# XCiT attention and RWKV channel mix on one core: crossbar transposes for v, q and k, norms as row sums, one buffer for x, a tanh gate

## Chip, cores, metric

The kernel runs on one core of a Trainium2 chip. The metric is the device time of one execution in microseconds; the time before is the median of three runs. A profile is one execution recorded by the hardware profiler. Engines are called PE (TensorE, matmuls; PEld its weight loads), DVE (VectorE), ACT (ScalarE), POOL (GpSimd) and SP (SyncE, which here only issues DMAs). The 16 DMA engines serve the queues of all of them.

## What is computed

Two stages. The first is a cross-covariance attention over channels: the norms and the product k^T q run over all 6208 tokens, and the softmax is only 256 by 256 per batch. Its output x = v a goes through a channel mix with a shift by one token.

```python
B, N, C = 4, 6208, 256                      # d_ff = 1024, tau = 1.0, float32 in and out
qn = q / (norm(q, axis=1) + 1e-6)           # a norm per channel, over all tokens
kn = k / (norm(k, axis=1) + 1e-6)
s  = kn.T @ qn / tau                        # per batch, 256 x 256
a  = softmax(s, -1)
x  = v @ a                                  # 6208 x 256

x_prev = x shifted down by one token (first row zero)
xk = mu_k * x + (1 - mu_k) * x_prev
xr = mu_r * x + (1 - mu_r) * x_prev
kk = relu(xk @ w_k) ** 2
out = sigmoid(xr @ w_r) * (kk @ w_v)
```

## The kernel before

**Tiling.** Tokens are cut into 12 blocks of 512 per batch (NB = 12, M = 512, S = 4 pieces of 128); 64 tokens per batch are left over (L = 64) and make one last block of 256 columns ("left"). There are 49 blocks in all. Matmuls take bf16 and accumulate in PSUM. Everything after the attention is held transposed, channels in partitions and tokens along the free dimension, so v must be transposed: x^T = a^T v^T.

**Norms and covariance.** For q and k a *group* g is 512 tokens of both, and a *unit* is 128 tokens of a group. `unit_matmul` (L115) adds a unit's k^T q into s_ps with two matmuls (L125). The squares of q and k are made on ACT (L113, or L108 for batch 0) and summed over tokens by matmuls with a matrix of ones, four at a time on strips of 32 columns (L131). `softmax_pieces` (L135) gathers the four strips with one more float32 matmul (L151), takes Sqrt on ACT (L152) and reciprocals on DVE (L156, L163), scales s, subtracts the row maximum, applies Exp with a sum as a second output (L177) and writes a_sb (L183). These eight pieces are put into the loop one per slot.

**Batch 0** is loaded in float32 on SP's queue (`group_load`, L86), q and k alternating, cast on DVE (L106) and squared on ACT (L108). Batches 1 to 3 are loaded by GpSimd's queue, which casts to bf16 (L100).

**The loop.** Blocks pass through a software pipeline. The loop over i from -2 to 48 has eight slots j; the order in which a slot issues its work is the order on each engine (the schedule is manual). In slot j of step i:

- `up(i + 1, j)`: two matmuls into kT_ps (L285) and a Relu to kr on ACT (L288); `square` (L294) makes kk on DVE one slot later.
- `down(i, j)`: for each 128 tokens the gate xr w_r (L309) and kk w_v (L313) into one vr_ps; `finish` applies Sigmoid on ACT (L321), multiplies on DVE (L322) and, after the fourth piece, SP stores 512 KB (L326).
- `x_half(i + 2, ...)` in slots 0 and 2: x^T (L230), copied to bf16 by ACT (L232). The tile xT has 513 columns; GpSimd copies the last column of the block before into the first (L225).
- `mix_delta`, `mix`: x - x_prev (L260), xk and xr (L270) on DVE.
- `v_load(i + 5)` on GpSimd's queue (L201); `v_transpose(i + 3)` in slot 6, eight PE transposes (L209); `v_evac` in slot 7, a DVE copy (L214).
- a `unit` of the next batch in slots 1, 3, 4, 5 and 7, until that batch's 49 units are done.

PSUM's eight banks: s_ps, ssq_ps, vT_ps, xT_ps, two kT_ps, two vr_ps.

Of the kernel before, what the change touches and what calls it, by code (L numbers as in the profile page):

```python
# [14 lines left out]
OP = mybir.AluOpType  # L15
# [3 lines left out]
def kernel(  # L19
# [23 lines left out]
    assert 0 < L < P  # L43
    G = NB * S
    inv_tau = 1.0 / float(tau)

# [3 lines left out]
    p2 = ctx.enter_context(tc.tile_pool(name="p2", bufs=3))  # L50
    ps = ctx.enter_context(tc.tile_pool(name="ps", bufs=1, space=bass.MemoryType.PSUM))
    ctx.enter_context(tc.manual_schedule())

# [4 lines left out]
    ones = const.tile([P, P], BF16, name="ones")  # L58
    nc.vector.memset(ones, 1.0)

    thirty2 = const.tile([P, P], F32, name="thirty2")
    nc.vector.memset(thirty2, 1.0 / 32)
# [6 lines left out]
    a_sb = const.tile([P, B, 2, C], BF16, name="a_sb")  # L69
    gate = const.tile([P, 1], BF16, name="gate")  # L70

    cov = {}
    groups = {}
# [4 lines left out]
    def qk_src(t, b, g):  # L81
        if g < NB:
            return t[b, :NB * M, :].rearrange("(p j) c -> p j c", p=P)[:, g * S:(g + 1) * S, :]
        return t[b, NB * M:, :].rearrange("(p j) c -> p j c", j=1)

    def group_load(b, g):  # L86
        rows, n = rows_of(g)
        qk = pq.tile([P, S, 2, C], BF16, name="qk", tag="qk", bufs=5)
        qk2 = pq.tile([P, S, 2, C], BF16, name="qk2", tag="qk2", bufs=3)
        groups[b, g] = (qk, qk2)  # L90
        if b == 0:
            t_f = []
            for i, t in enumerate((q, k)):
                f = pq.tile([P, S, C], F32, name=f"f{i}", tag=f"f{i}", bufs=6)
                nc.sync.dma_start(f[:rows, :n], qk_src(t, b, g))
                t_f.append(f)
            groups[b, g] += tuple(t_f)
        else:
            for i, t in enumerate((q, k)):
                nc.gpsimd.dma_start(qk[:rows, :n, i, :], qk_src(t, b, g))  # L100

    def group_cast(b, g):
        rows, n = rows_of(g)
        qk, qk2, *t_f = groups[b, g]
        for i in range(2):
            nc.vector.tensor_copy(qk[:rows, :n, i, :], t_f[i][:rows, :n])  # L106
        for i in range(2):
            nc.scalar.activation(qk2[:rows, :n, i, :], t_f[i][:rows, :n], AF.Square)  # L108

    def unit_square(b, g, s):  # L110
        rows, _ = rows_of(g)
        qk, qk2 = groups[b, g][:2]
        nc.scalar.activation(qk2[:rows, s], qk[:rows, s], AF.Square)  # L113

    def unit_matmul(b, g, s):  # L115
        rows, n = rows_of(g)
        t0 = g == 0 and s == 0
        te = g == NB
        if t0:
            cov[b] = (ps.tile([P, 2, C], F32, name="s_ps", tag="s_ps"),  # L120
                      ps.tile([P, 2 * C], F32, name="ssq_ps", tag="ssq_ps"))
        s_ps, ssq_ps = cov[b]
        qk, qk2 = groups[b, g][:2]
        for ih in range(2):
            nc.tensor.matmul(s_ps[:, ih, :], qk[:rows, s, 1, ih * P:(ih + 1) * P],  # L125
                             qk[:rows, s, 0, :], start=t0 and ih == 0, stop=te,
                             skip_group_check=True)

        if s == n - 1:
            for u in range(n):  # L130
                nc.tensor.matmul(ssq_ps[32 * u:32 * (u + 1)], ones[:rows, :32],  # L131
                                 qk2[:rows, u].rearrange("p i c -> p (i c)"),
                                 start=g == 0, stop=te if u == 0 else g == NB - 1, tile_position=(0, 32 * u))

    def softmax_pieces(b):  # L135

        s_ps, ssq_ps = cov.pop(b)
        nrm = pn.tile([P, 2 * C], F32, name="nrm")
        junk = pn.tile([P, P], F32, name="junk")
        rk = pn.tile([P, 2], F32, name="rk")  # L140
        rq = pn.tile([P, C], F32, name="rq")
        s_sb = pn.tile([P, 2, C], F32, name="s_sb")
        mx = pn.tile([P, 2], F32, name="mx")
        sm = pn.tile([P, 2], F32, name="sm")

        def a():
            nc.vector.tensor_copy(nrm, ssq_ps)

        def a2():
            all_ps = ps.tile([P, 2 * C], F32, name="all_ps", tag="ssq_ps")  # L150
            nc.tensor.matmul(all_ps, thirty2, nrm, start=True, stop=True)  # L151
            nc.scalar.activation(nrm, all_ps, AF.Sqrt)  # L152

        def b1():
            nc.vector.tensor_scalar_add(nrm[:, :C], nrm[:, :C], 1e-6)
            nc.vector.reciprocal(rq, nrm[:, :C])  # L156

        def b2():
            for ih in range(2):
                nc.vector.scalar_tensor_tensor(junk, nrm[:, C + ih * P:C + (ih + 1) * P], 1.0, ident_f,  # L160
                                               op0=OP.mult, op1=OP.mult, accum_out=rk[:, ih:ih + 1])
            nc.vector.tensor_scalar_add(rk, rk, 1e-6)
            nc.vector.reciprocal(rk, rk)  # L163
            if inv_tau != 1.0:
                nc.vector.tensor_scalar_mul(rk, rk, inv_tau)
# [310 lines left out]
```

## Time and profile before

| | |
|---|---|
| median of three runs | 581.26 us (578.61 to 582.14) |
| span of the profiled execution | 579.8 us |
| PE busy | 528.0 us (91%) |
| ACT busy | 451.7 us (78%) |
| DVE busy | 443.6 us (77%) |
| POOL busy | 126.9 us (22%) |
| DMA, queue q0 (GpSimd's, casting) | 32.98 MB, 46.3% of 16 engines' span |
| DMA, queue q1 (SP's) | 38.15 MB, 18.4% |
| mean granted PE clock | 0.975 |

The profiled execution's time is known by its span, from the first to the last instruction. Busy time is the time with at least one instruction of the engine under way; matmuls overlap, so a step in starts, not the length of one, tells what they cost. A view in order of time has start, length, engine, line, operation and tiles; in brackets stands idle time ahead of it and what ended that. Bytes of q0 are counted as written, in bf16; it reads twice as many.

### The profile page before, as it was taken

What the parts mean: (1) busy time and instruction counts of PE and PEld (TensorE: products, weight loads), DVE (VectorE), ACT (ScalarE), POOL (GpSimd) and SP (SyncE); (2) the same over time, 40 slices, a digit from 0 to 9 for tenths busy, and PEclk for the clock granted to TensorE, in tenths of its full rate; (3) what the DMA queues carried; (4) which work ended last, traced back from release to release, by engine and by line L of the source; (5) the groups of instructions that cost most, each with busy time, mean ns of one, the idle gap of its engine ahead of it and who ended that gap; (6) DMA issues with size and microseconds to landing.
All of it is one profiled execution on the core that took longest, in us unless ns stands there. A gap on an engine that the chain in (4) does not pass through costs nothing.

```text
span 579.8 us, 10793 instructions
## 1 busy us (share of the span) xinstructions
PE 528.0 (91%) x3920; PEld 350.9 (61%) x3920; DVE 443.6 (77%) x977; ACT 451.7 (78%) x895; POOL 126.9 (22%) x188
## 2 busy tenths in 40 slices
PE   4574999999889999999979999999979999999996
PEld 2331466666546666666646666666646666666765
DVE  4535788777798777777888777786789898888984
ACT  6845888888878888788887888887877777767774
POOL 0064233223121324313202323321101111110000
PEclk9955999999989999999999999999999999999999
DMA  8999979858538888957729687964222444522122
GB/s 329 415 267 196 135 111 143 151 84 124 102 54 151 129 145 130 133 110 109 111 55 183 93 130 127 148 103 100 57 54 58 108 73 94 105 60 73 37 74 90
DMA packets 95684, 71.80 MB, mean 124 GB/s; under 512 B 3980, under 2 KB 92304, under 8 KB 95632
## 3 DMA queue, kind: packets, MB, share of 16 engines
q0 software_dynamic: 65808, 32.98, 46.3%
q1 hardware_dynamic: 29824, 38.15, 18.4%
q8 instruction: 30, 0.49, 0.3%
q14 instruction: 22, 0.18, 0.1%
HBM read 78.65 MB, written 25.43 MB: 180 GB/s over the span
## 4 chain that ended last, share of the span: by engine, by line
PE 80%; DVE 9%; DMA 6%; ACT 3%; issue 1%; SPq 0%; ACTq 0%; DVEq 0%
PE kT_ps L285 27%; PE vr_ps L313 27%; PE xT_ps L230 7%; PE vr_ps L309 7%; PE s_ps L125 5%; PE vT_ps L209 4%; PE ssq_ps L131 2%; DMA f_185<-in_k_dram 2%; DMA f_273<-in_k_dram 2%; DVE kk L294 2%; DMA f_347<-in_k_dram 2%; DVE xk L270 1%; DVE rq L156 1%; DVE res L322 1%; ACT kr L288 1%
## 5 line engine op out<-in xcount | busy, mean ns | idle before, releaser
L288 ACT ACTIVATE kr<-kT_ps 128x512 bf16<-128x512 f32 (+1 forms) x392 | 232.8, 596 | 55.9 <-PE kT_ps L285 22.7
L313 PE MATMUL vr_ps<-w_v_sb,kk 128*128 128x256 bf16 x1552 | 233.8, 273 | 7.2 <-DVE kk L294 7.0
L285 PE MATMUL kT_ps<-xk,w_k_sb 128*128 128x512 bf16 (+1 forms) x784 | 232.9, 379 | 5.1 <-ACT kr L288 4.0
L313 PEld LDWEIGHTS <-kk 128*128 128x128 bf16 x1552 | 152.1, 98 | 66.6 <-DVE kk L294 8.3
L294 DVE TENSOR_TENSOR kk<-kr 128x512 bf16<-128x512 bf16 (+1 forms) x392 | 153.0, 417 | 1.9 <-ACT kr L288 1.4
L322 DVE TENSOR_TENSOR res<-res,vr_ps 128x256 f32<-128x256 f32 x194 | 81.6, 421 | 82.2 <-ACT res L321 81.8
L285 PEld LDWEIGHTS <-w_k_sb 128*128 128x128 bf16 x784 | 71.7, 98 | 44.1 <-issue 17.1
L125 PE MATMUL s_ps<-qk 128*128 128x256 bf16 x392 | 73.0, 287 | 18.3 <-DVE qk L106 18.3
L232 ACT CAST xT<-xT_ps 128x512 bf16<-128x512 f32 x96 | 56.5, 588 | 35.3 <-PE xT_ps L230 35.3
L321 ACT ACTIVATE res<-vr_ps 128x256 f32<-128x256 f32 x194 | 74.2, 382 | 7.6 <-PE vr_ps L313 7.1
L225 POOL COPY xT<-xT 128x2 bf16<-128x2 bf16 x44 | 28.0, 637 | 221.7 <-issue 174.0
L309 PE MATMUL vr_ps<-w_r_sb,xr 128*128 128x256 bf16 x388 | 74.2, 273 | 0.0
L270 DVE SCALAR_TENSOR_TENSOR xr<-delta,mu_r_t,xT 128x512 bf16<-128x512 bf16 x96 | 71.8, 748 | 0.0
L270 DVE SCALAR_TENSOR_TENSOR xk<-delta,mu_k_t,xT 128x512 bf16<-128x512 bf16 x96 | 71.6, 747 | 0.0
L230 PE MATMUL xT_ps<-vT,a_sb 128*128 128x512 bf16 x192 | 58.2, 385 | 11.2 <-DVE a_sb L183 7.8
L309 PEld LDWEIGHTS <-xr 128*128 128x128 bf16 x388 | 38.0, 98 | 44.9 <-issue 0.6
L201 POOL DMA_DIRECT2D v_bf<-in_v_dram x48 | 36.3, 757 | 113.8 <-DVE kk L294 92.1
L125 PEld LDWEIGHTS <-qk 128*128 128x128 bf16 x392 | 38.6, 102 | 31.4 <-DVE qk L106 22.1
L260 DVE TENSOR_TENSOR delta<-xT 128x1024 bf16<-128x1024 bf16 x48 | 33.3, 693 | 20.1 <-ACT xT L232 19.4
L100 POOL DMA_DIRECT2D qk<-in_q_dram x39 | 29.1, 747 | 52.9 <-PE s_ps L125 10.9
L214 DVE COPY vT<-vT_ps 128x1024 bf16<-128x1024 bf16 x48 | 32.9, 686 | 4.0 <-PE vT_ps L209 4.0
L209 PE MATMUL vT_ps<-ident,v_bf 128*128 128x128 bf16 x384 | 30.1, 223 | 0.8 <-DVE vT L214 0.8
(192 smaller groups left out, 313.7 us busy)
## 6 DMA issues: line engine op xcount, KB each, us to landing
out_dram<-res SPq DMA_DIRECT2D x48, 512.0 KB, 3.8
v_bf<-in_v_dram POOLq DMA_DIRECT2D x48, 256.0 KB, 4.4
qk<-in_q_dram POOLq DMA_DIRECT2D x36, 256.0 KB, 4.6
qk<-in_k_dram POOLq DMA_DIRECT2D x36, 256.0 KB, 6.4
f_93<-in_q_dram SPq DMA_DIRECT2D x1, 512.0 KB, 3.8
f_95<-in_k_dram SPq DMA_DIRECT2D x1, 512.0 KB, 4.8
f_117<-in_q_dram SPq DMA_DIRECT2D x1, 512.0 KB, 5.6
f_119<-in_k_dram SPq DMA_DIRECT2D x1, 512.0 KB, 6.7
```

What stands on the lines that cost most here:

```text
L125: nc.tensor.matmul(s_ps[:, ih, :], qk[:rows, s, 1, ih * P:(ih + 1) * P], qk[:rows, s, 0, :], start=t0 and ih == 0, stop=te, skip_group_che ...
L209: nc.tensor.transpose(vT_ps[:, ch, s * P:(s + 1) * P], v_bf[:, s, ch * P:(ch + 1) * P], ident)
L230: nc.tensor.matmul(xT_ps, a_sb[:, b, ih, dh * P:(dh + 1) * P], vT[:, ih, :], start=ih == 0, stop=ih == 1)
L232: nc.scalar.copy(xT[:, dh, 1:], xT_ps)
L270: nc.vector.scalar_tensor_tensor(o[:, dh], st[i, "d"][:, dh], mu[:, dh:dh + 1], st[i, "x"][:, dh, :M], op0=OP.mult, op1=OP.add)
L285: nc.tensor.matmul(kT_ps[:, :m], w_k_sb[:, dh, fh * P:(fh + 1) * P], xk[:, dh, :m], start=dh == 0, stop=dh == 1)
L288: nc.scalar.activation(kr[:, :m], kT_ps[:, :m], AF.Relu)
L294: nc.vector.tensor_tensor(st[i, "kk"][:, fh, :m], kr[:, :m], kr[:, :m], op=OP.mult)
L309: nc.tensor.matmul(vr_ps[:, D:], xr[:, dh, s * P:(s + 1) * P], w_r_sb[:, dh, :], start=dh == 0, stop=dh == 1)
L313: nc.tensor.matmul(vr_ps[:, :D], kk[:, fh, s * P:(s + 1) * P], w_v_sb[:, fh, :], start=fh == 0, stop=fh == 7)
L321: nc.scalar.activation(res[:, s], vr_ps[:, D:], AF.Sigmoid)
L322: nc.vector.tensor_tensor(res[:, s], res[:, s], vr_ps[:, :D], op=OP.mult)
```

## The change

The whole kernel body is rearranged around five edits; the arithmetic of the channel mix is the same.

1. **Transposes by DMA.** v blocks 2 to 47 are transposed from SBUF to SBUF with `dma_start_transpose` on SP's queue (`v_transpose_dma`, slot 1 of step i for block i + 4) and not on PE; `v_evac` is gone. Blocks 0 and 1 still use PE, with a DVE copy. q and k of batches 1 to 3 are transposed the same way, 128 x 2048 at a time (`group_transpose`), one group ahead of its first unit, and the left-over tokens of v too.
2. **Norms as row sums.** With channels in partitions, the sum over tokens of a unit is one ACT Square with `accum_out` over 128 x 512 elements. The matmuls with ones go for batches 1 to 3. The square root is a `pow` on GpSimd, the reciprocal is taken on 128 x 4 numbers, and q's factors come into the free dimension by a store to DRAM and a broadcast load. The row maximum is not subtracted (for |1/tau| up to 60); k's factor is the scale of Exp. s_ps is copied out by ACT when the batch's last unit is in.
3. **x of a batch in one buffer X**, 128 x 2 x 6145, so the column before a block is there already.
4. **Tanh gate.** sigmoid(z) = (1 + tanh(z/2))/2; the half is multiplied into w_v_sb once, on DVE. The gate has a PSUM bank of its own (g_ps), Tanh works on two pieces (128 x 512) at a time, and the finish is one scalar_tensor_tensor per two pieces.
5. **Batch 0's order.** q first, then q and k interleaved, k's last piece in parts of 2, 1 and 1; norms by matmuls with one column of ones; q's factor is ready before the last k pieces; v of block 0 comes in float32 on SP's queue.

The units are placed by a table `due`: the 49 units of batch 1 over 61 slots from step 0, those of batches 2 and 3 over 96 slots each. PSUM after: one bank for xT, g and s, two for v, three for kT. Output tiles share eight buffers (f4) with the float32 loads; v_bf, vT and batch 0's q share thirteen (b2).

The core of the diff:

```diff
+    X = const.tile([P, 2, 1 + NB * M], BF16, name="X")
+    nc.vector.memset(X[:, :, 0:1], 0.0)
...
+    def root(src, n):
+        a = pn.tile([P, 4], F32, name="nrm_a")
+        if len(src.shape) == 3:
+            nc.vector.tensor_reduce(a[:, :n], src, axis=AX, op=OP.add)
+        else:
+            nc.vector.tensor_copy(a[:, :n], src)
+        r = pn.tile([P, 4], F32, name="nrm_r")
+        nc.gpsimd.tensor_tensor(r[:, :n], a[:, :n], half[:, :n], op=OP.pow)
+        return r
...
+    def v_transpose_dma(i):
         v_bf = st.pop((i, "v"))
-        vT_ps = ps.tile([P, 2, M], BF16, name="vT_ps", tag="vT_ps")
-        for ch in range(2):
-            for s in range(S):
-                nc.tensor.transpose(vT_ps[:, ch, s * P:(s + 1) * P], v_bf[:, s, ch * P:(ch + 1) * P], ident)
-        st[i, "vTp"] = vT_ps
-
-    def v_evac(i):
-        vT = p2.tile([P, 2, M], BF16, name="vT", tag="vT", bufs=2)
-        nc.vector.tensor_copy(vT, st.pop((i, "vTp")))
-        st[i, "vT"] = vT
+        vT = new_vT(i)
+        nc.sync.dma_start_transpose(vT.rearrange("p s h t -> p (s h) t"), v_bf.rearrange("p s c -> p (s c)"))
...
-        nc.scalar.copy(xT[:, dh, 1:], xT_ps)
+        nc.scalar.copy(X[:, dh, 1 + t * M:1 + (t + 1) * M], xT_ps)
...
+    def gate_act(i, u):
+
+        if (i, "g", u) in st:
+            nc.scalar.activation(st[i, "res"][:, 2 * u:2 * u + 2], st.pop((i, "g", u)), AF.Tanh, scale=0.5)
...
-        nc.scalar.activation(res[:, s], vr_ps[:, D:], AF.Sigmoid)
-        nc.vector.tensor_tensor(res[:, s], res[:, s], vr_ps[:, :D], op=OP.mult)
...
+        nc.vector.scalar_tensor_tensor(r, r, 1.0, st.pop((i, "v", u)), op0=OP.add, op1=OP.mult)
...
+    def group_transpose(b, g):
+
+        rows, n = rows_of(g)
+        qk = groups[b, g]["qk"]
+        T = pq.tile([P, 2, S, 2, P], BF16, name="qkT", tag="qkT", bufs=3)
+        groups[b, g]["T"] = T
+        if n == S:
+            nc.sync.dma_start_transpose(T.rearrange("p i s h t -> p (i s h) t"), qk.rearrange("p i s c -> p (i s c)"))
...
+    def unit(b, g, s):
...
+        for ih in range(2):
+            nc.tensor.matmul(cov[b][:, ih, :], qk[:rows, 1, s, ih * P:(ih + 1) * P], qk[:rows, 0, s, :],
...
+        for u in ([s] if n == S else range(S)):
+            i, h = divmod(u, 2)
+            junk = pn.tile([P, S, P], BF16, name="junk")
+            nc.scalar.activation(junk[:, :n, :rows], G["T"][:, i, :n, h, :rows], AF.Square,
+                                 accum_out=ssq[b][:, u, g:g + 1])
...
+        def bcast_out():
+            d = pd.tile([2, P], F32, name="rq_d")
+            hold["d"] = d
+            with nc.allow_non_contiguous_dma(reason="256 words"):
+                nc.sync.dma_start(d.rearrange("h p -> p h"), hold["r"][:, 0:2])
+
+        def bcast_in():
+            rq_bc = pn.tile([P, C], F32, name="rq_bc", bufs=1)
+            hold["bc"] = rq_bc
+            nc.sync.dma_start(rq_bc, hold["d"].rearrange("h p -> (h p)").unsqueeze(0).to_broadcast([P, C]))
...
+        return [a, None, a2, bcast_out, bcast_in, None, None, None, None, c, e, None, f]
...
+    for ih in range(2):
+        soft_half(0, ih, t_sb, rk, e_sb, sm, mx)
+    v_load(1)
     nc.gpsimd.dma_start(w_r_sb, moe_w_r.rearrange("(ko ki) d -> ki ko d", ki=P))
     nc.gpsimd.dma_start(w_v_sb, moe_w_v.rearrange("(fo fi) d -> fi fo d", fi=P))
+    nc.vector.tensor_scalar_mul(w_v_sb, w_v_sb, 0.5)
     v_load(2)
...
+    for h in range(2):
+        v_transpose_pe(0, v0, 2 * h, 2 * h + 2, "v")
+    for ih in range(2):
+        soft_scale(0, ih, e_sb, sm)
...
+            if j == 1 and 2 <= i + 4 < LAST:
+                v_transpose_dma(i + 4)
+            if j == 2 and 3 <= i + 5 < LAST:
                 v_load(i + 5)
...
+            for u in due.get(T, []):
+                b, g, s = units[u]
+                at = (b - 1) * (NB + 1) + GORD.index(g)
+                while pos["load"] < min(len(loads), at + 4):
+                    group_load(*loads[pos["load"]])
+                    pos["load"] += 1
+                while pos["T"] < min(len(loads), at + 2):
+                    group_transpose(*loads[pos["T"]])
+                    pos["T"] += 1
+                unit(b, g, s)
```

## The prediction, on record before the change was run

> **What bounds the kernel now.** I read the page first, then the busy times by stage, then the up-projection's matmuls by stage, then single instructions in order of time, then the DMA queues. Lines of the page, with the profiled execution's span of 579.8 us in its head:
>
> ```profile
> PE 528.0 (91%) x3920; PEld 350.9 (61%) x3920; DVE 443.6 (77%) x977; ACT 451.7 (78%) x895; POOL 126.9 (22%) x188
> ...
> PE   4574999999889999999979999999979999999996
> ...
> ACT  6845888888878888788887888887877777767774
> ...
> PEclk9955999999989999999999999999999999999999
> ...
> PE 80%; DVE 9%; DMA 6%; ACT 3%; issue 1%; SPq 0%; ACTq 0%; DVEq 0%
> ```
>
> TensorE holds 80% of the chain of waits at the full granted clock, except in a head of some 66 us (clock 0.5 in slices 3 and 4) and in three dips. Busy time by stage (columns: us; busy us and instructions of PE, PEld, DVE, ACT, POOL; clock; DMA share; GB/s):
>
> ```profile
> 80.00:140.00 60.00, 58.90 (x456) 39.97 (x457) 44.86 (x98) 50.05 (x106) 18.51 (x26) 1.00 0.75 124
> 440.00:560.00 120.00, 118.97 (x885) 81.95 (x883) 105.74 (x236) 89.52 (x183) 13.91 (x20) 1.00 0.33 76
> 150.00:180.00 30.00, 25.85 (x174) 16.05 (x174) 25.31 (x61) 22.86 (x44) 5.28 (x9) 0.94 0.47 79
> ```
>
> Stages with q/k units (first row) and without them (second) are full of matmuls; the third, a softmax, is not. The matmuls into kT_ps alone are a meter of progress, 16 to a block:
>
> ```profile
> 180.00:260.00 80.00, 35.48 (x120) 1.00 0.79 131
> 280.00:310.00 30.00, 11.51 (x40) 1.00 0.50 85
> 310.00:390.00 80.00, 36.08 (x122) 1.00 0.81 131
> 410.00:440.00 30.00, 11.03 (x38) 1.00 0.30 59
> 440.00:560.00 120.00, 62.38 (x210) 1.00 0.33 76
> ```
>
> With five units a block takes 80/(120/16) = 10.7 us, without units 120/(210/16) = 9.15 us. The three softmax stages run 38 (150 to 180 us), 40 and 38 matmuls where 52.5 would fit without units: (14.5 + 12.5 + 14.5)/52.5 x 30 = **23.7 us lost in the softmaxes**. So what TensorE no longer does is worth its time, as long as nothing else takes over.
>
> **Part 1, TensorE work removed.** Two stretches in order of time:
>
> ```profile
> 105.16 0.38 PE L125 MATMUL s_ps<-qk 128*128 128x256 bf16 x2
> ...
> 105.48 0.40 PE L131 MATMUL ssq_ps<-qk_687,ones 128*32 128x512 bf16 x4
> ...
> 105.81 0.61 PE L285 MATMUL kT_ps<-xk,w_k_sb 128*128 128x512 bf16 x2
> ...
> 464.69 0.61 PE L209 MATMUL vT_ps<-ident,v_bf 128*128 128x128 bf16 x8
> ...
> 465.14 0.59 PE L285 MATMUL kT_ps<-xk,w_k_sb 128*128 128x512 bf16 x2
> ```
>
> Starts count, since matmuls overlap. Eight v transposes take 465.14 - 464.69 = 0.45 us; 46 blocks lose them: **-20.7 us**. A pair of s_ps matmuls costs 0.21 us (2 x 0.107), so the norm matmuls hold the engine from 105.37 to 105.81, 0.44 us a group; of the 39 groups of batches 1 to 3, some 34 lie in the full loop: **-15.0 us**. The first ten units, done in the head before, now start at i = 0: +10 x 0.21 = **+2.1 us**. Blocks then cost 9.15 - 0.45 = 8.70 us without units and 8.70 + 4.08 x 0.21 = 9.57 us with 49 units in twelve blocks. Batch 1 has its 49 units in 61 slots, 6.4 a block: 10.05 us.
>
> **Part 2, ScalarE.** The norms become one Square with accum_out per unit. Accumulation shows only at Exp, plain Squares beside it:
>
> ```profile
> 50.78 0.51 ACT L177 ACTIVATE s_sb<-s_sb,mx 128x256 f32<-128x256 f32 x1 [4.14 <-DVE mx L173]
> 51.19 0.19 ACT L177 ACTIVATION_READ_ACCUMULATOR s_sb<-s_sb,mx 128x1 f32 x1
> 51.29 0.49 ACT L177 ACTIVATE s_sb<-s_sb,mx 128x256 f32<-128x256 f32 x1
> ...
> 54.07 1.67 ACT L113 ACTIVATE qk_379<-qk 128x512 bf16<-128x512 bf16 x3
> ```
>
> Three Squares in 1.67 us with a last one of 0.63 follow at (1.67 - 0.63)/2 = 0.52 us. Accumulation adds between nothing and 0.2 us (the reader is 0.19); I take 0.2, so 0.72 a unit. Relu (0.60 long) and the x copy (0.59) are followed 0.50 and 0.48 us later; a tanh of 128x512 is like a Relu. Per block: 8 x 0.50 + 2 x 0.48 + 2 x 0.50 = 5.96, plus 4.08 x 0.72 = 2.94, in all 8.9 us against TensorE's 9.57: hidden, but 93% full. In batch 1 it is 5.96 + 6.4 x 0.72 = 10.6 against 10.05. I charge 0.6 x 7.6 blocks and 0.1 x 24 blocks for jitter: **+7 us** (0 to +34, the upper end with no overlap of instructions, worked out below). Tanh halves the count of gate instructions (194 sigmoids at 0.38), and the finish on VectorE becomes 97 of some 0.75 (the nearest row is the 128x512 scalar_tensor_tensor, 0.748) for 194 at 0.421. VectorE loses the v evacuations (0.69 a block): about 87% full at 8.70, covered by TensorE.
>
> **Part 3, softmax.** The profile has 16 ACT_TABLE_LOADs of 1.283 us, ahead of each batch's Sqrt, its Exp and the Sigmoids after them; Sqrt goes to GpSimd as pow and Sigmoid becomes tanh. Also gone: the 128x256 reciprocal (1.75 us), two float matmuls (0.99 us a batch), max and its reduction. In their place come tiny instructions, spread over 13 slots, and a trip of 256 floats through DRAM on SP's queue. Of 23.7 us lost I leave 8 (0 to 24): **-16 us**. The bcast load must land in five slots, some 5.5 us; DMAs of 64 KB land in a median 2.0 us here, 512 KB in 3.8. The Trainium skill, "ScalarE: Activation LUTs", section Table sets, puts tanh and exp into one set and sqrt into another, so no reload should be left; were they apart, 6 loads (7.7 us of ScalarE) would stay in the loop.
>
> **Part 4, the head.** q and k of batch 0 are still 12.7 MB; the last cast starts at 35.87 us, and the first x matmul only at 52.51. That chain of 16.6 us gets short (no table loads, q's norm ready early, last k piece in quarters). But a new wait takes part back: VectorE's multiplication of w_v_sb by 0.5 stands ahead of the v evacuation and the a_sb scaling, so these wait for the w_v DMA, and x for them. GpSimd issues w_v after the pow that needs the last k, at about 38.3 us. Casting DMAs move at most:
>
> ```profile
> GB/s 351 394 410 415 420 408 334 236 232 214 227 197 189 195 200 193 197 197 196 198 193 197 197 195 197 194 198 194 195 199 196 197 197 197 195 196 197 196 195 204
> ```
>
> (28 to 60 us.) Block 1's v, w_r and w_v are 0.92 MB from 36.3 us on: 4.7 us at 196 GB/s and 2 us to land (the 64 KB row), and a rest of w_k, so 44.5 us (41 to 49.4, the latter with the 11.1 us that w_v takes now). Add 1.3 for the multiplication (twice the 0.69 of a 128x1024 copy), 0.75 for v and 0.87 for a_sb: x at 47.4, 5 us earlier. The first block ahead of the loop gains another 1.5 without units in it. **-6.5 us** (-13 to 0).
>
> **Part 5, the rest.** One buffer X removes 44 GpSimd copies (28.0 us busy, and the loads no longer queue behind them); delta waited 0.6 us for them: nothing. Later v loads are covered by a lead of five blocks.
>
> **Part 6, the crossbar transposes.** All go through SP's queue, behind the output stores (0.37 us each to issue). A transpose waits there for its load, and stores behind it wait too; eight f4 buffers cover that. Bytes: 36 x 524 KB + 46 x 262 KB + small ones = 31.3 MB, per block 0.80 MB in batches 2 and 3, 1.1 MB in batch 1. No row shows a crossbar. Bounds by the nearest rows: plain hardware DMAs moved 418 GB/s at 10 to 20 us, casting ones 196; from the other side, a packet takes 18.4% x 579.8 x 16/29824 = 57 ns in q1, and if every 256-byte run of 128 elements costs a packet, 16 engines do 16 x 256/57 ns = 72 GB/s. Need: 0.80/9.6 us = 84 GB/s, and 1.1/10.7 = 103 in batch 1. Low end: hidden. I take the casting row, as the transposes too change what is written: 1.1 MB take 5.6 us of 10.7, **0 us**; Squares wait on ScalarE if this cover goes, then the Relus behind them, then TensorE.
>
> The skill's "DMA: Bandwidth & Descriptors", section Latency and other measured facts, has 261 GB/s for transposes: 4.2 us a block, hidden too. The same page speaks against the change in its section on why a DMA increments its semaphore by 16: a transpose between SBUF places took earlier generations 262,144 cycles for 8,192 tiles, 32 a tile. Were a tile 256 bytes, 122,000 tiles would take an estimated 3.3 ms at the 1.2 GHz that "Trainium Kernel Development and Optimization", section NeuronCore Architecture, gives for the sync engine; were it 4 KB, 0.2 ms, spread over the loop.
>
> **Sum.** 579.8 - 20.7 - 15.0 + 2.1 + 7 - 16 - 6.5 = 530.7 us of span. The runs' median, 581.26, is 1.5 above the span: **532 us**.
>
> **Rivals.** (a) The transposes bind: every 256-byte run a packet of 57 ns. A block then takes 0.80 MB/72 GB/s = 11.1 us in batches 2 and 3, and 15.4 in batch 1: +1.5 x 24 + 4.7 x 7.6 = +72, **604 us**. For it: q1's packets cost 57 ns though they carry 1.28 KB. Against: those packets are also limited by bytes. It decides below about 84 GB/s, and eats the whole gain near 75. (b) ScalarE becomes the bound: instructions that don't overlap cost 8 x 0.60 + 2 x 0.59 + 2 x 0.60 + 4.08 x 0.82 = 10.5 us a block, and 12.4 in batch 1. That is +0.9 x 24 + 1.6 x 7.6 = +34 over rows without my charge, so 532 - 7 + 34 = **559 us**. For it: 93% full, in order, with x copies that wait for matmuls (35.3 us in all now). Against: three kT_ps buffers let TensorE run ahead. (c) All softmax waits go and the head gains 13: 532 - 8 - 6.5 = **517 us**.
>
> **Chances.** Forecast 0.58, (a) 0.21, (b) 0.11, (c) 0.06, and 0.04 for a transpose rate that just cancels the gain. The forecast's own range is 518 to 550. Leaving out most of (a) and a little below, 510 to 596. Within 1%, about what a measurement here can tell from no change: 0.04. Faster 0.75, slower 0.21.
>
> **What would show it.** Right: the clock at 0.9 or more after the head, kT_ps matmuls at 16 per 8.7 us after the last unit and 9.6 before, one or two table loads, VectorE waiting for w_v near 44 us, x near 47. Wrong: Squares released by a DMA into qkT (a), gaps of TensorE ended by Relu with ScalarE over 95% busy (b), or an x matmul waiting for vT.

## The result, and the profile after

The changed kernel takes 623.98 us (621.76 to 625.65, four runs) against 581.51 us beside it: **slower by 7.3%** (ratio 1.0729, 95% interval 1.0695 to 1.0763). The forecast was 532 us, and 623.98 also lies above its range. The profiled execution has a span of 622.0 us; the sum of the prediction was 530.7, so 91.3 us are to be explained.

The page of the changed kernel:

```profile
PE 498.7 (80%) x3480; PEld 339.4 (55%) x3538; DVE 391.6 (63%) x810; ACT 436.0 (70%) x952; POOL 87.5 (14%) x144
...
PE   3754791955879169999989089999996699999996
...
ACT  6752690926779069999879089989983577777773
...
PEclk9975996785998669999999679999999799999999
DMA  8989999999999999999999999999929786523222
...
q1 hardware_dynamic: 157088, 70.38, 55.5%
q0 software_dynamic: 37632, 32.74, 40.3%
...
PE 58%; DMA 26%; ACT 4%; issue 2%; DVE 2%; SPq 2%; POOL 0%; ACTq 0%; DVEq 0%
```

Every engine but the DMAs has less to do than before: TensorE 498.7 us busy for 528.0. But its row now has holes down to 0 and 1, the granted clock is lower in the slices with holes, and the DMA row is at 9 without a break until the last transposes of q and k. In the chain DMA rose from 6% to 26%. Queue q1 carries 157,088 packets for 29,824 before. Busy time by stage (columns as in the prediction's rows; the DMA share passes 1 here, as packets of one engine overlap in the count):

```profile
80.00:140.00 60.00, 38.23 (x252) 26.02 (x255) 25.72 (x51) 31.53 (x79) 8.90 (x15) 0.82 1.19 154
440.00:560.00 120.00, 107.67 (x732) 72.86 (x744) 89.89 (x188) 87.26 (x171) 9.96 (x13) 0.96 0.64 112
```

In batch 0's blocks (where batch 1's q and k are loaded and turned; called batch 1's stage here) TensorE is busy 38 of 60 us. Before, the same window had 58.9, with a DMA share of 0.75. Who waits for whom (us in total, times, longest):

```profile
POOL v_bf L199 <- DMA vT<-v_bf: 58.9, 6, 17.8
ACT e_sb L174 <- DVE t_sb L415: 52.9, 3, 20.8
DVE t_sb L415 <- DMA rq_bc<-rq_d: 51.1, 3, 20.1
...
ACT junk L379 <- DMA qkT<-qk: 49.2, 9, 16.8
PE v_ps L318 <- DVE kk L294: 48.3, 4, 18.6
```

ScalarE waits 49.2 us for transposes of q and k at its Squares (junk), and 52.9 us at three Exps, behind VectorE, which waits for the broadcast of q's factors. Relus stand behind both; so kk is late, and with it TensorE. SP's queue around the first softmax, in order of time:

```profile
192.98 0.37 SPq L407 DMA_DIRECT2D rq_d<-nrm_o  x1
195.65 0.38 SPq L335 DMA_DIRECT2D out_dram<-res  x1
196.15 13.47 SPq L211 DMA_TRANSPOSE vT<-v_bf  x1
209.72 0.55 SPq L412 DMA_DIRECT2D rq_bc<-rq_d  x1
210.44 11.45 SPq L361 DMA_TRANSPOSE qkT<-qk  x1
```

The second column is the time to *issue*. A transpose of v holds the queue for 13.47 us, and the broadcast load stands behind it. It went out at 209.72, and VectorE could start at 222.03, 20.12 us after its last instruction; nothing in that chain is work.

Where the 91 us lie is read from the starts of the output stores, one a block. The first store of the kernel before, then the first, ninth and 33rd of the changed kernel:

```profile
78.51 0.41 SPq L326 DMA_DIRECT2D out_dram<-res  x1
```

```profile
83.14 0.50 SPq L335 DMA_DIRECT2D out_dram<-res  x1
...
226.03 0.38 SPq L335 DMA_DIRECT2D out_dram<-res  x1
...
490.08 0.37 SPq L335 DMA_DIRECT2D out_dram<-res  x1
```

The first is at 83.14 (forecast 78.51 before - 6.5 = 72.0): 11 us. From the first to the ninth store, batch 1's stage with its softmax, 142.9 us pass for 8 x 10.05 + 2.7 = 83.1: 60 us. From the ninth to the 33rd, 264.1 for 24 x 9.57 + 5.3 = 235.0: 29 us. From there on the forecast holds. The three make 100; the 7 us that the prediction charged for ScalarE lie in them too, which leaves 93.

### The profile page after: what moved, and what is told of

It reads as the page before. It is cut to its first block, busy times and chain, and to the rows that moved or that the text cites. A ratio compares the mean times of both kernels' runs of the same rounds, so it can differ in the third digit from the quotient of the medians.

```text
span 622.0 us, 9910 instructions
## 1 busy us (share of the span) xinstructions
PE 498.7 (80%) x3480; PEld 339.4 (55%) x3538; DVE 391.6 (63%) x810; ACT 436.0 (70%) x952; POOL 87.5 (14%) x144
## 3 DMA queue, kind: packets, MB, share of 16 engines
q1 hardware_dynamic: 157088, 70.38, 55.5%
## 4 chain that ended last, share of the span: by engine, by line
PE 58%; DMA 26%; ACT 4%; issue 2%; DVE 2%; SPq 2%; POOL 0%; ACTq 0%; DVEq 0%
PE v_ps L318 22%; PE kT_ps L285 20%; DMA qkT<-qk 17%; PE g_ps L304 6%; PE xT_ps L230 6%; DMA rq_bc<-rq_d 5%; PE s_ps L374 3%; DMA rq_d<-nrm_o 2%; SPq L211 2%; ACT junk L379 1%; ACT kr L288 1%; DMA w_v_sb<-in_moe_w_v_dram 1%; ACT res L324 1%; ACT X L232 1%; DVE kk L294 0%
## 5 line engine op out<-in xcount | busy, mean ns | idle before, releaser
L318 PE MATMUL v_ps<-w_v_sb,kk 128*128 128x256 bf16 x1552 | 239.0, 277 | 48.9 <-DVE kk L294 48.3
L379 ACT ACTIVATE junk<-qkT 128x512 bf16<-128x512 bf16 (+1 forms) x156 | 94.8, 611 | 49.2 <-DMA qkT<-qk 49.2
L304 PE MATMUL g_ps<-w_r_sb,xr 128*128 128x256 bf16 x388 | 75.2, 276 | 20.3 <-ACT res L324 18.6
L232 ACT CAST X<-xT_ps 128x512 bf16<-128x512 f32 x96 | 56.9, 592 | 26.8 <-PE xT_ps L230 26.8
L304 PEld LDWEIGHTS <-xr 128*128 128x128 bf16 x388 | 38.3, 99 | 68.2 <-issue 25.8
L270 DVE SCALAR_TENSOR_TENSOR xr<-delta,mu_r_t,X 128x512 bf16<-128x512 bf16 x96 | 71.5, 745 | 0.0
L270 DVE SCALAR_TENSOR_TENSOR xk<-delta,mu_k_t,X 128x512 bf16<-128x512 bf16 x96 | 71.4, 744 | 0.0
L331 DVE SCALAR_TENSOR_TENSOR res<-res,v_ps 128x512 f32<-128x512 f32 x97 | 65.9, 679 | 1.5 <-ACT res L324 1.5
L324 ACT ACTIVATE res<-g_ps 128x512 f32<-128x512 f32 x97 | 58.1, 599 | 0.9 <-PE g_ps L304 0.9
L374 PE MATMUL s_ps<-qk 128*128 128x256 bf16 (+1 forms) x294 | 57.4, 278 | 0.0
L199 POOL DMA_DIRECT2D v_bf<-in_v_dram x47 | 36.1, 773 | 63.9 <-DMA vT<-v_bf 58.9
L174 ACT ACTIVATE e_sb<-t_sb,nrm_o 128x256 f32<-128x256 f32 x8 | 4.0, 500 | 54.0 <-DVE t_sb L415 52.9
L259 DVE TENSOR_TENSOR delta<-X 128x1024 bf16<-128x1024 bf16 x48 | 32.9, 686 | 3.0 <-ACT X L232 3.0
```

The costliest lines, as they stand in the source:

```text
L232: nc.scalar.copy(X[:, dh, 1 + t * M:1 + (t + 1) * M], xT_ps)
L270: nc.vector.scalar_tensor_tensor(o[:, dh], st[i, "d"][:, dh], mu[:, dh:dh + 1], X[:, dh, c:c + M], op0=OP.mult, op1=OP.add)
L304: nc.tensor.matmul(g_ps[:, s % 2], xr[:, dh, s * P:(s + 1) * P], w_r_sb[:, dh, :], start=s % 2 == 0 and dh == 0, stop=dh == 1, skip_group_ ...
L318: nc.tensor.matmul(v_ps[:, s % 2], kk[:, fh, s * P:(s + 1) * P], w_v_sb[:, fh, :], start=s % 2 == 0 and fh == 0, stop=fh == 7, skip_group_ ...
L324: nc.scalar.activation(st[i, "res"][:, 2 * u:2 * u + 2], st.pop((i, "g", u)), AF.Tanh, scale=0.5)
L331: nc.vector.scalar_tensor_tensor(r, r, 1.0, st.pop((i, "v", u)), op0=OP.add, op1=OP.mult)
```

## The experiments

The theories, by their short names. **Turns**: the DMA engines take packets of the queues in turn, so the crossbar's 256-byte packets lose against the casting loads' long ones. **Bytes**: the crossbar's own rate is the limit. **Engine time**, which replaced bytes after experiment 5: each transfer needs so many microseconds of the 16 engines, and the sum of all is more than a block has. **Queue**: the softmax's trip through DRAM, stuck on SP's queue, is the cause by itself. Kernels without an interval ran once, beside a run of the kernel before (581.9 to 583.4 us).

**1. Short casting runs.** In the changed kernel the tile of q and k holds q's 512 tokens and then k's, so a casting load writes 2 KB at a stretch (before: 512 bytes).

```diff
-        qk = pq.tile([P, 2, S, C], BF16, name="qk", tag="qk", bufs=5)
+        qk = pq.tile([P, S, 2, C], BF16, name="qk", tag="qk", bufs=5)
```

> Edit: the q/k tile is laid out [P, S, 2, C] again, so a casting load writes runs of 512 bytes and not of 2048; the same bytes are loaded and transposed. Theory 'turns' (the DMA engines take turns between queues packet by packet, so a 256-byte crossbar packet of 18 ns waits for a 2048-byte casting packet of 172 ns, or 60 ns if it has 512 bytes): beside loads the transposes get 256 B x 16/(18 + 60 ns) = 52 GB/s and not 256 B x 16/(18 + 172 ns) = 22 GB/s, so transposes land in some 5 us, and most of the 90 us of stalls goes: 560 to 590 us. Theory 'bytes' (the crossbar's own rate is the limit): 615 to 630 us, or longer, as four packets of 60 ns cost more engine time than one of 172. Theory 'queue' (the trip of q's factors through DRAM, stuck on SP's queue behind transposes, is the main loss): batch 1 stays at 16 us a block, above 600 us.

618.62 us (span 616.9): 5 us won, little more than the 3.9 us by which the changed kernel's four runs differ. The transposes of q and k issue in the same time (median 4.5 us for 4.3), and the softmaxes still cost some 13 to 15 us each. By itself the packet size is not the cause. But the small gain is a difference of larger ones: from the first to the ninth store 124.5 us pass for 142.9, from there to the 33rd 273.9 for 264.1, and the first store comes 2.8 us later. In batch 1's stage short runs help by 18 us, in batches 2 and 3 they cost 10.

**2. q's factors by a float32 matmul**, no trip through DRAM.

```diff
-                nc.sync.dma_start(d.rearrange("h p -> p h"), hold["r"][:, 0:2])
+                nc.vector.tensor_scalar_mul(hold["dq"][:, h], ident_f, hold["r"][:, h:h + 1])
...
-            nc.sync.dma_start(rq_bc, hold["d"].rearrange("h p -> (h p)").unsqueeze(0).to_broadcast([P, C]))
+            nc.tensor.matmul(bc_ps, ones_f, hold["dq"].rearrange("p h d -> p (h d)"), start=True, stop=True)
+            nc.vector.tensor_copy(rq_bc, bc_ps)
```

> Edit: for batches 1 to 3 q's factors get into the free dimension by a float32 matmul of ones with a diagonal (as batch 0 does), not by the store to DRAM and the broadcast load on SP's queue; slots are unchanged. Theory 'queue': the stalls at the three softmaxes (20.8 + 18.6 + 12.8 = 52 us over a steady block of 9.6) go: 570 to 580 us. Theory 'turns' or 'bytes': the transposes are as late as before, so part of the 52 us comes back as Squares waiting for qkT: 585 to 605 us. Batch 1's blocks stay near 16 us in all of them.

608.34 us. The 51 us of waiting for rq_bc are gone, but only 15.6 us of the time: the Squares' waits for qkT rise from 49.2 to 81.8 us. One cover was lifted, and the next wait lay under it. The Squares' rows, in the changed kernel and in this one:

```profile
L379 ACT ACTIVATE junk<-qkT 128x512 bf16<-128x512 bf16 (+1 forms) x156 | 94.8, 611 | 49.2 <-DMA qkT<-qk 49.2
```

```profile
L379 ACT ACTIVATE junk<-qkT 128x512 bf16<-128x512 bf16 (+1 forms) x156 | 94.6, 608 | 81.8 <-DMA qkT<-qk 81.8
```

**3. No transposes of q and k.** The Squares read the tile as loaded, so the norms are sums over other numbers; v and the trip through DRAM stay as they are.

```diff
-                    group_transpose(*loads[pos["T"]])
...
-            nc.scalar.activation(junk[:, :n, :rows], G["T"][:, i, :n, h, :rows], AF.Square,
+            nc.scalar.activation(junk[:rows, :n, :], qk[:rows, i, :n, h * P:(h + 1) * P], AF.Square,
```

> Edit: the q/k transposes are left out and the Squares read the q/k tile as it lies (so the norms are not the sums over tokens); instruction counts on TensorE, ScalarE and VectorE are unchanged, v is still transposed by DMA, and the trip through DRAM stays. 'turns' and 'bytes': all waits for qkT go, SP's queue is free, batch 1 runs at 10.7 us a block and the trip lands in its five slots: 535 to 550 us, near the 532 predicted. 'queue' alone: the trip is short now too, as only v's transposes are ahead: the same. What it tells is whether anything beyond the transposes of q and k is lost: more than 555 us would mean so.

586.53 us, not 535 to 550. Batch 1's blocks fall from 16 us to 10.4 on average, as expected. But the three softmaxes lose 28, 16 and 13 us: the waits for rq_bc are still 53.1 us, as v's transposes (up to 13.9 us to issue) stand ahead of the load:

```profile
L416 DVE TENSOR_TENSOR t_sb<-s_sb,rq_bc 128x512 f32<-128x512 f32 x3 | 2.1, 692 | 53.1 <-DMA rq_bc<-rq_d 53.1
```

So two mechanisms, not one: q's and k's transposes spoil batch 1, the queue ahead of a small load spoils the softmaxes.

**4. v on TensorE for all blocks**, transposes of q and k by the crossbar.

```diff
-                v_transpose_dma(i + 4)
+                v_transpose_pe(i + 4, st.pop((i + 4, "v")), 0, S, "v")
```

> Edit: v is transposed by TensorE for all blocks (eight transposes and a 128x1024 copy on VectorE in slot 1), q and k still by DMA. TensorE pays 46 x 0.45 = 21 us where it is full. 'bytes': the crossbar moves 12.1 of 31.3 MB less, which takes off a third or more of the 90 us of stalls: 590 to 615 us. 'turns': the q/k transposes run beside the same casting loads, batch 1 stays above 13 us a block: 610 to 635 us. 'queue': no 13 us v transpose stands ahead of the broadcast load any more, so half of the 52 us at the softmaxes goes: 600 to 615 us.

603.34 us: waits for qkT 26.2 us and for rq_bc 28.8, both lower, none gone; steady blocks (equal steps from store to store, no DMA late) 10.0 us for 9.6. The time fits what bytes and queue had expected, batch 1's blocks (14.7 us on average) what turns had.

**5. The DMAs alone.** All computing is left out: eight groups of casting loads (0.52 MB written each), eight 128 x 2048 transposes, each alone and together, with one read by VectorE behind each; then plain float32 loads and broadcast loads.

> Not the attention at all: the DMA kinds of the changed kernel by themselves and in pairs, in stages kept apart by copies on VectorE. In order: the 1 KB store and one broadcast load; 8 groups of casting q/k loads (2048-byte runs); 8 transposes of 128x2048; both together; the same with 512-byte runs; 16 plain float32 loads of 512 KB from ScalarE's queue; these with 8 transposes; 4 broadcast loads; 8 groups of casting loads with 4 broadcast loads. 'bytes' (the crossbar is slow in itself): 8 transposes (4.2 MB) alone need 40 us or more, under 100 GB/s. 'turns' (slow only beside packets of another queue): alone 18 to 25 us (170 to 235 GB/s), beside casting loads with long runs 2 to 4 times as long, with short runs less than 1.5 times, beside plain 4 KB packets as bad as beside long casting runs. 'slot' (the broadcast load itself is slow, whatever is beside it): a broadcast load of 128 KB alone takes 8 us or more; else it lands in some 3 us alone and over 8 only beside casting loads.

VectorE's reads (tok) of the transposed tiles alone, in order of time, the first two and the last:

```profile
45.55 0.15 DVE L69 CAST tok<-turn 128x1 f32<-128x1 bf16 x1 [4.16 <-DMA turn<-src]
48.02 0.15 DVE L69 CAST tok<-turn 128x1 f32<-128x1 bf16 x1 [2.32 <-DMA turn<-src]
...
62.81 0.15 DVE L69 CAST tok<-turn 128x1 f32<-128x1 bf16 x1 [2.21 <-DMA turn<-src]
```

One in 2.47 us, 524 KB: 212 GB/s. The crossbar is not slow, and the casting loads alone need about as much, 2.6 us a group. Together, with runs of 2 KB (started at 64.49) and then of 512 bytes (at 110.61):

```profile
91.77 0.15 DVE L69 CAST tok<-cast 128x1 f32<-128x1 bf16 x1 [1.88 <-DMA cast<-in_q_dram]
91.87 0.15 DVE L69 CAST tok<-turn 128x1 f32<-128x1 bf16 x1
94.68 0.15 DVE L69 CAST tok<-turn 128x1 f32<-128x1 bf16 x1 [2.65 <-DMA turn<-src]
...
108.75 0.15 DVE L69 CAST tok<-turn 128x1 f32<-128x1 bf16 x1 [2.19 <-DMA turn<-src]
...
146.86 0.15 DVE L69 CAST tok<-cast 128x1 f32<-128x1 bf16 x1 [4.54 <-DMA cast<-in_q_dram]
146.96 0.46 DVE L69 CAST tok<-turn 128x1 f32<-128x1 bf16 x4
...
157.09 0.15 DVE L69 CAST tok<-turn 128x1 f32<-128x1 bf16 x1 [2.30 <-DMA turn<-src]
```

Bytes falls: alone the eight transposes take 21.9 us, not 40. *Engine time* holds for this pair: together they need 108.75 - 64.49 = 44.3 us, the sum of 22.3 and 21.9 alone; with short runs 46.5, or 5.8 us a pair. *Turns* shows in the order: when the 2 KB loads were done, one transpose of eight had landed (some 0.52 MB in 27 us, 19 GB/s); beside 512-byte runs four had (58 GB/s). But it had also expected the last transpose sooner with short runs, and that came no sooner.

Beside plain float32 loads the sum does not come out. In order: the casting loads with transposes (2 KB runs), 16 plain loads of 512 KB alone, and these with eight transposes (columns: us; busy us and instructions of DVE, POOL; clock; DMA share; GB/s):

```profile
64.00:109.00 45.00, 3.51 (x60) 8.47 (x16) 1.00 1.08 186
...
159.00:182.00 23.00, 3.59 (x44) 0.00 (x0) 1.00 0.95 365
183.00:238.00 55.00, 3.86 (x60) 0.00 (x0) 1.00 1.08 229
```

The plain loads take 23.6 us alone, from the first issue to the last read, and with the transposes 55.0, some 9.5 more than the sum of both. Why is open.

**6. Neither transposes of q and k nor the DRAM trip** (edits 2 and 3 together, norms as in 3).

> Edit: both earlier edits at once: no transposes of q and k (the Squares read the tile as it lies, so the norms are not the sums over tokens), and q's factors spread by a matmul and not through DRAM. v is still transposed by DMA. If the two are all that was lost beyond the head, the stalls of 37.9, 25.5 and 22.8 us that were left at the softmaxes go to about 12 each: 586.5 - 28 - 16 - 13 = 530 us, 530 to 540. If v's transposes beside casting loads are a cause of their own, stalls at the batch changes stay: over 550 us.

549.97 us, between what was expected with v's transposes harmless (530 to 540) and with them as a cause of their own (over 550). The softmaxes cost at most 2 us each; what is left are single blocks of 13 to 15 us, in which v's transposes come late.

**7. The whole result without those two.** The norms go back to TensorE, as matmuls with one column on a Square of the untransposed tile; q's factors as in 2; w_v is halved later, behind the scaling of a_sb. kT_ps has two buffers.

```diff
-            nc.scalar.activation(junk[:, :n, :rows], G["T"][:, i, :n, h, :rows], AF.Square,
-                                 accum_out=ssq[b][:, u, g:g + 1])
+        nc.scalar.activation(sq[:rows], qk[:rows, :, s, :], AF.Square)
...
+            nc.tensor.matmul(ssq[b][:, u:u + 1], sq[:rows, i, h * P:(h + 1) * P], ones_b[:rows],
+                             start=first("n"), stop=True, skip_group_check=True)
```

> Edit: full result. q's and k's norms by TensorE, four matmuls of each unit's squares with one column of ones (some 0.045 us each), q's factors spread by a matmul, two kT banks and not three, and w_v's halving moved behind the a_sb scaling. v by DMA, X, the tanh gate and batch 0's order stay. TensorE: 8.70 + 4.08 x (0.21 + 0.18) = 10.3 us a block for 24 blocks, 8.70 + 6.4 x 0.39 = 11.2 in batch 1. Against the 532 of the prediction: +0.7 x 24 + 0.5 x 7.6 = 553 us (545 to 565) if q/k's transposes and the trip through DRAM are the cause; above 580 if something else in the change is.

567.54 us, 2.5 above the expected range. x's first matmul is now at 45.56 us (52.61 in the changed kernel), but the first store still at 83.26: TensorE then waits 8.05 us for the first vT. SP's queue in batch 2's blocks, some 45 us behind the first softmax, where blocks take up to 13.5 us for 10.0:

```profile
211.09 11.40 SPq L211 DMA_TRANSPOSE vT<-v_bf  x1
223.92 0.37 SPq L335 DMA_DIRECT2D out_dram<-res  x1
224.39 11.75 SPq L211 DMA_TRANSPOSE vT<-v_bf  x1
```

**8. Norms added up by GpSimd**, in float32 on 128 x 512, otherwise as 7, but with three buffers for kT_ps.

```diff
+        nc.gpsimd.tensor_tensor(ssq[b][:rows], ssq[b][:rows], sq[:rows], op=OP.add)
```

> Edit: full result. As the kernel with norms on TensorE, but GpSimd adds each unit's squares into one float32 tile, and four matmuls per batch sum that over the rows; three kT banks. TensorE 9.57 us a block, ScalarE 5.96 + 4.08 x 0.52 = 8.1, GpSimd one 128x512 addition a unit. If an addition takes under 2 us (4.08 in 9.57 us, or 6.4 in 10.05) it is hidden: 530 to 545 us. If it takes longer, GpSimd sets the pace: with 3 us, 12 us a block.

635.89 us, the slowest of all, and a miss by 90. The adds take 1.31 us each. But what hurts is VectorE beside them; first the changed kernel's row, then this one's:

```profile
L294 DVE TENSOR_TENSOR kk<-kr 128x512 bf16<-128x512 bf16 x384 | 160.0, 421 | 136.4 <-ACT kr L288 131.0
```

```profile
L294 DVE TENSOR_TENSOR kk<-kr 128x512 bf16<-128x512 bf16 x384 | 242.7, 644 | 98.8 <-ACT kr L288 97.8
```

A square on VectorE takes 644 ns on average instead of 421, and most blocks of batches 2 and 3 take 10.6 to 13.6 us. Kernel 8 by itself shows that the adds do it: from 220 to 480 us, beside them, a square takes 751 ns; from 510 to 600, when none is left, 420.

**9, 10, 11. What is left in 7: v.** On TensorE until block 33 (9, first diff); casting runs of 512 bytes as in 1 (10); or v loaded up to seven blocks ahead instead of five and turned up to six instead of four (11, second diff).

```diff
+                if i + 4 < 34:
+                    v_transpose_pe(i + 4, st.pop((i + 4, "v")), 0, S, "v")
```

```diff
-            if j == 1 and 2 <= i + 4 < LAST:
-                v_transpose_dma(i + 4)
+            if j in (1, 4) and vp["t"] < min(i + 7, LAST) and (vp["t"], "v") in st:
+                v_transpose_dma(vp["t"])
+                vp["t"] += 1
```

> The kernel with q/k norms by one-column matmuls, q's factor by a float matmul and w_v halved later (565.8 us of span, steady blocks of 10.0 with q/k units and 8.7 without), and now v turned by TensorE and copied out by VectorE for the blocks before 34, by the crossbar after that, when no casting load of q or k is left. 'The crossbar starves beside casting loads': no wait for vT until block 34, none of SP's transposes over 3 us to issue, the first store near 75 instead of 83.3, blocks of 10.0 + 0.45 = 10.5 where the crossbar kernel has 10.0 to 13.9, so a mean of 10.6 over the same 24 blocks instead of 10.58: 556 to 568 us, little won in all, since 31 blocks pay 0.45 us of TensorE for stalls of 32 us. 'The stalls belong to the softmax itself and not to the transposes': the blocks at the softmaxes keep their 12 to 14 us and the time is 575 or more.

> The same 565.8-us kernel with the q/k tile laid out with q and k beside each other in every row, so that the casting loads write runs of 512 bytes instead of 2 KB; v by the crossbar throughout. 'The engines take packets in turn, so what a transpose gets goes with the other side's packet size': transposes of v issue in some 5 us instead of 10 to 12 during the loads, the waits for vT fall from 24.4 us to under 10, and the time to 548 to 560; the loads take longer (some 4.5 us for 0.5 MB) but still land within their lead of four groups. 'Only the bytes count': issue times and waits as before, 563 to 570.

> The same 565.8-us kernel with v loaded up to seven blocks ahead instead of five and turned up to six blocks ahead instead of four; nothing else. 'The transposes are late only in bursts, while four groups of q and k are loaded at once': two blocks more of lead (20 us) cover a backlog of 2 to 3 us a block; the waits for vT in the loop vanish but for the first, at 60 to 68 us, which no lead covers, and the time falls to 543 to 553. 'They lack rate over whole batches': the backlog only starts later, 558 to 566.

553.13, **537.4** and 548.5 us. All three take the stalls out of the blocks; ahead of them TensorE still waits once, 8.3 us for a load of v in 9 and 3.4 and 10.0 us for the first vT in 10 and 11. In kernel 9 the steady block is 10.4 us for 10.0, and with 32 blocks of TensorE transposes it ends 15.8 us behind kernel 10. Kernels 9 and 10 beat what was expected. SP's issues of v's transposes (min, median and longest ns), first in 7 and then in 10:

```profile
L211 SPq DMA_TRANSPOSE vT<-v_bf x46: 1341/2045/11750, 54.0 to 520.5; - x46
```

```profile
L211 SPq DMA_TRANSPOSE vT<-v_bf x46: 1397/1858/4923, 52.9 to 490.3; - x46
```

Same bytes, other packets: the longest issue falls from 11.75 to 4.92 us, waits for vT from 24.4 to 3.4 us, and the loads themselves land sooner (q's median 6.0 us for 9.1). Turns expects this, engine time does not: the loads even take more of it (q0 has 49.7% of the span for 43.2%). Nor is it the new layout of the tile: the Squares that read it take 627 ns in both. Kernel 11 shows that lead also covers it, though its transposes still issue in up to 16.3 us, and the first vT still comes late.

**12, 13. The best version timed, and the change with all of its parts.** 12 is kernel 10 again. 13 is the changed kernel with its transposes of q and k and its row sums, and the three repairs (short runs, q's factors by matmul, w_v later).

> The kernel of 535.6 us of span once more (norms by one-column matmuls, q's factor by a float matmul, w_v halved later, 512-byte casting runs, v by the crossbar), for an interval against the kernel before. All theories: 536 to 539 us, ratio 0.918 to 0.930.

> The changed kernel with all of its parts kept, the crossbar transposes of q and k and ScalarE's row sums too, and the three lossy places mended together: 512-byte casting runs, q's factor by a float matmul, w_v halved later. 'The engine time adds up': batch 1 needs 1.6 x (2.5 + 2.45) + 1.2 + 1.3 + 1.3 = 11.7 us of DMA time a block and stays bound by it, 12 to 14 us a block; batches 2 and 3 need 1.02 x 4.95 + 3.8 = 8.9 and run at 9.6 to 10.2; softmaxes cost some 3 us each: 540 to 560. 'q's and k's transposes starve whatever the others' packets are': blocks of 14 in batch 1 and stalls of over 10 us at two of three softmaxes as with short runs alone, 568 to 585.

Kernel 12: 536.37 us (534.43 to 536.78, five runs), ratio 0.9213, 95% interval 0.9185 to 0.9241: **7.9% faster** than the kernel before. Its TensorE and DMA rows:

```profile
PE   2695899999999999999999999999999999999995
...
DMA  8989999999799999979599999983389575424113
```

Kernel 13: 593.71 us, and both expectations missed it, on the high side. Its DMA row and the largest wait for a DMA:

```profile
DMA  8979999999999999999999999999737976542222
```

```profile
ACT junk L379 <- DMA qkT<-qk: 83.7, 25, 9.9
```

The DMAs are full again, and the Squares wait 83.7 us, now in 25 pieces of up to 9.9 us. No softmax stands out by over 8 us. The expectation added up what each transfer takes alone; with the 5.8 us that a pair takes together (experiment 5), batch 1 needs 1.6 x 5.8 + 3.8 = 13.1 us a block; 14.3 were measured. Batches 2 and 3 need 1.02 x 5.8 + 3.8 = 9.7; they had 10.8. The last 1.1 us a block are not explained; each block also stores 512 KB of plain float32, and experiment 5 shows that plain transfers beside transposes can cost more than the sum.

## Why the prediction was wrong

Kernels 13 and 12 split the miss. The three repairs bring the span from 622.0 to 591.9 (30 us, nearly all of it between the first and the ninth store: in batches 2 and 3 the softmaxes' stalls go, but the other blocks grow from 9.6 to some 10.4 us); taking out q's and k's transposes, with the norms on TensorE, brings it to 532.7 (59 us, of which 12 lie before the first store, 27 in batch 1's stage and 20 in batches 2 and 3).

**Part 6 failed, and most with it.** It charged 0 us for the transposes; taking out q's and k's was worth 59. It set a rate against a need, and took the rate as if the 16 engines were free. They were not: the views of before that it quotes show shares of 0.75 to 0.81 in the stages with units. The term should have been engine time, added to what is there: in batch 1 some 1.6 x 2.47 + 1.2 us of transposes, on top of 1.6 x 2.6 us of loads, 1.3 of v and 1.3 of stores (an estimate: 0.5 MB of float32 loads took 1.28 us in experiment 5), 11.9 us for a block of 10.05. That is not the whole: a block of batch 1 took 16.1 us on average until the first softmax, where 44.3/8 = 5.5 us a pair gives 12.7. Short runs alone brought it to 14.3 (experiment 1), which puts some 2 us down to turns; the rest is open. The casting row (196 GB/s) that it took was close to what the crossbar does alone (212), so the number was right and its use wrong. Rival (a) named the place, and its sign, Squares released by a DMA into qkT, was there (49.2 us). The prediction counted 122,000 packets rightly (122,240 of q1's have 256 bytes). That (a) came out near the result (604) is luck: 16 x 256 bytes over 57 ns are 72 GB/s, and alone the crossbar does 212; and the 11.1 us that it gave each block of batches 2 and 3 were 9.6 outside the softmaxes.

The figure of the Trainium skill that spoke against the change ("DMA: Bandwidth & Descriptors", section Why a DMA increments its semaphore by 16 and not by 1), 262,144 cycles of the sequencer for 8,192 tiles on earlier generations, is not borne out if a tile is a run of 256 bytes: eight transposes with 16,384 such runs took 21.9 us alone, 1.3 ns a run. The page's 261 GB/s (section Latency and other measured facts) is nearer to the 212 measured alone; what a transpose gets beside other loads was lower still (19 and 58 GB/s). The same page, section Queues, rings and completion order, says that each engine goes round the queues packet by packet; kernels 7 and 10 fit that, with 30 us between two packet sizes.

**Part 3 was right on the work, wrong on the trip.** One table load is left of 16. The load was given five slots, some 5.5 us, and taken to land in them; the store took a median of 12.2 us to land, the load 11.0, and at the first softmax a transpose of v held the queue for 13.5 between them. It cost 20, 18 and 13 us of waiting on VectorE. The prediction said that the load must land within five slots and that stores stand behind transposes, but did not put the two together. Undone alone it was worth 15.6 us (experiment 2), as the Squares' wait lay behind.

**Part 4 named the right wait and got its size wrong.** w_v was put at 44.5 us; it came at 50.74:

```profile
50.74 0.69 DVE L469 TENSOR_SCALAR w_v_sb<-w_v_sb 128x2048 bf16<-128x2048 bf16 x1 [7.69 <-DMA w_v_sb<-in_moe_w_v_dram]
...
52.61 0.61 PE L230 MATMUL xT_ps<-vT,a_sb 128*128 128x512 bf16 x1 [10.53 <-DVE a_sb L179]
```

GpSimd issued it at 43.76, not 38.3, as the pow ahead of it waited for k's norm until 41.6, and two more loads were issued between; it landed 7.0 us later. So x came at 52.61 instead of 47.4, as late as before. (The prediction's last cast, at 35.87, is that of the last whole piece; two of 64 rows follow, the second at 36.88.) The halving took 0.69 us for the 1.3 forecast. Halved later, x starts at 45.15 (kernel 12); the first store came sooner only when v's transposes did too.

**Parts 1 and 2 were right, but for a sum.** Where no DMA is late, blocks with units are 9.6 us apart in the changed kernel (9.57 forecast), and 8.7 without (8.70). In experiment 3 ScalarE does the same row sums and blocks stay at 9.6, and 10.4 on average in batch 1: rival (b) fell. Its sum was also wrong: 12.4 us in batch 1 are 2.4 above 10.05, not 1.6, which makes it 565 us, not 559. v on the crossbar saves 0.45 us of TensorE a block, as forecast: with v on TensorE the steady block is 10.0 for 9.56 (experiment 4) and 10.41 for 9.96 (kernel 9). **Part 5** held for X; that "later v loads are covered" was true of the loads, not of the transposes behind them: 24.4 us of waits for vT in kernel 7.

That the best version ends at 532.7 us of span, 2.0 from the sum, is partly chance: it pays 0.4 us more a block with units (10.0 for 9.57) for norms on TensorE, while nothing shows of the 7 us charged for ScalarE and little of the 8 left to the softmaxes (a step of 11.3 us at the first two, for 10.0), and x starts 2.2 us earlier than forecast.

## What to carry to other kernels

Price a DMA that is "hidden" in engine time, and add it to the share that the stage's DMA row already shows; in a stage at 0.75 a rate measured alone is not what it gets. Even that sum came out low here: blocks took 1 to 3 us more. Look at the packet sizes of whatever runs beside a crossbar transpose, and shorten the neighbour's runs before moving the transpose back: here that was a change of one tile's layout, worth 30 us between kernels 7 and 10, but only 5 in the changed kernel, whose DMAs had no time to spare. And a small transfer on a critical chain must not queue behind a long issue: a matmul of 128 x 256 replaced the trip through DRAM.

## What the runs showed of the hardware

- Crossbar transposes of 128 x 2048 bf16 alone: 2.47 us, 212 GB/s; while casting loads in 2 KB runs last some 19 GB/s, in 512-byte runs some 58 (experiment 5).
- SP's issue of a transpose of v took 1.3 us at the shortest and up to 13.5 us in the changed kernel, 16.3 in kernel 11, and everything behind it on SP waits.
- A broadcast of one DRAM row to 128 partitions landed after 3.4 us on idle engines and 6.2 to 12.1 beside casting loads; a store of 256 single words took 8.8 us even alone (experiment 5).
- GpSimd's float32 adds slow VectorE: 421 to 644 ns for a bf16 square on average (experiment 8). "GPSIMD Engine Reference" of the Trainium skill, section Specifications, says that the two share their SBUF interfaces, with contention for VectorE instructions with two SBUF inputs, among others. The runs agree: the square reads SBUF, and the finish, with one input in PSUM, stays at 676 ns for 680.
